# 1/den of a linear attention: from broadcasts into 32 partitions to broadcasts into all 128 from four stored copies

## Chip, cores and metric

The kernel runs on one core of one Trainium2 chip. The metric is device time in microseconds (us) for one execution; the time before is the median of three runs.

## What is computed

A block of a transformer, for 2048 rows of width 1024: a layer norm with a modulation taken from a conditioning vector `c`, linear attention with 32 heads of 32 columns, a residual sum, a second modulated layer norm, a gated feed-forward part of inner width 3584, and a second residual sum. The change lies in the attention:

```python
phi = lambda t: jnp.where(t > 0, t + 1, jnp.exp(t)) + 1e-06
pq, pk = (phi(q), phi(k))
kv = jnp.einsum('bhsd,bhse->bhde', pk, v)
z = jnp.einsum('bhsd->bhd', pk)
num = jnp.einsum('bhqd,bhde->bhqe', pq, kv)
den = jnp.einsum('bhqd,bhd->bhq', pq, z)[..., None] + 1e-06
o = num / den
return (lambda x, *d: x.transpose(*d))(o, 0, 2, 1, 3).reshape(B, S, D) @ wo
```

`den` is one number for each head and row. Inputs and outputs are bf16.

## The kernel before

The 2048 rows are 16 chunks of 128 (`NCH`) in four groups of 512 (`sg`, 0 to 3). The 1024 columns are eight groups of 128 (`g`, 0 to 7), each with four heads of 32 columns. `PQ[sg]` holds phi(q) transposed: its 128 partitions are the columns of one head group, so that partition 32k to 32k+31 belongs to head k of the group; its free dimensions are `g` and the row.

1/den is needed in that layout: the same value on the 32 partitions of a head. The kernel gets it in these steps.

- `den(pr_, b)` (L1233 on) treats two row groups together (`pr_` 0: groups 0 and 1; 1: groups 2 and 3). TensorE multiplies `PQ` by a masked `z` into one PSUM bank, VectorE adds 1e-6 (L1245) and takes the reciprocal into `RDC` (L1246). `RDC` has 128 partitions of 256 f32, one kilobyte each. A DMA stores it to the DRAM tensor `scr_rd` (L1248).
- `rb_load(sg, hs)` (L1255) reads it back for a row group, half by half (`h`; half a group is 256 rows). For each head of a group, one DMA reads a row of 8 KB (eight head groups of 256 f32) and writes it to 32 partitions of `RB[sg % 2]`: four DMAs of 256 KB for each half, 32 in all (L1260).
- `pq_scale(sg, h, gs)` (L1268) multiplies `PQ` by `RB` in place on VectorE, two head groups at a time (L1273), four multiplies for each half.
- `wo_mm` (L1283) multiplies the scaled `PQ` by `W2`, the product of kv and the output weights; VectorE adds the residual (L1291).

Before `wo_mm` TensorE works through 24 tiles of pk times the normalised input (`m_tile`, L895). When the third tile of a head group is evacuated by ScalarE (L900), `m_t(g)` transposes it by DMA (L703, into `mtb`), `kv_prod(g)` multiplies it on TensorE (L913), VectorE masks the result into `kvt` (L920), and `w2_pair(i)` makes `W2` for two head groups on TensorE (L1201), copied by ScalarE and VectorE (L1208).

The order on TensorE and on the DMA queue of SyncE (SP) is that of the program. A table `HOOK` says after which tile a step is put:

```python
HOOK = {0: "ga", 6: "kv0", 10: "kv1", 11: "w0", 13: "kv2", 15: "modp kv3 z32", 16: "den0", 17: "w1 rb0.0 rb0.1", 18: "",
        19: "kv4", 20: "den1 ps0.0", 21: "gbr", 22: "ps0.1", 23: "rb2.0"}
```

After the tiles come the rest of the loads (`rb_load(1)`, `rb_load(2, (1,))`, L1356 and L1357), then the chunks of `wo_mm`, and between these the loads and multiplies of row group 3 and the steps of the second layer norm (`SLOT`).

The order on VectorE, ScalarE and GpSimd between two marks of the program (L1050 and L1765) is chosen by a planner, `reorder` (L244): it computes a due time for every operation backwards, from estimated costs and the dependencies, DMAs included, and then places the ready operation that is due first. Dependencies between operations, through SBUF, PSUM or stated by hand, become semaphore waits. The DMAs of SP use eight semaphores in turn, and each DMA waits for the one eight places before it.

Of the kernel before, what the change touches and what calls it, by code (L numbers as in the profile page):

```python
# [10 lines left out]
P = 128  # L11
# [3 lines left out]
NSG = 4  # L15
CPG = NCH // NSG
SGW = P * CPG
NDC = D // P
NG = 8
HPG = 4  # L20
# [310 lines left out]
def bass_adaLN_cond__linear_attn_block__geglu_ffn__prompt_kernel(  # L331
# [12 lines left out]
    bf16, f32, f32r, i32 = dt.bfloat16, dt.float32, dt.float32r, dt.int32  # L344
# [1 line left out]
    scr_mod = nc.dram_tensor("scr_mod", [2, NDC, P], f32).ap()  # L346
    scr_y = nc.dram_tensor("scr_y", [4 * CPG, P, NDJ, 2 * P], bf16).ap()
    scr_x = nc.dram_tensor("scr_x", [P, NCH, D], bf16).ap()
    scr_rd = nc.dram_tensor("scr_rd", [NSG, 2, HPG, NG, SGW // 2], f32).ap()
    with ExitStack() as es:  # L350
        es.enter_context(nc.allow_non_contiguous_dma(reason="1024 modulation values, laid out by partition"))
        arena = es.enter_context(nc.sbuf_tensor("arena", [P, ARENA_BYTES], dt.uint8, align_bytes=64))
# [4 lines left out]
        def at(name, shape, dty, off):  # L357
            return nc.alloc_sbuf_tensor_at(name, shape, dty, offset=ABASE + off, align_bytes=4)
# [39 lines left out]
        RB = [at(f"rb{i}", [P, 2, NG, SGW // 2], f32, OFF_RB[i]) for i in range(2)]  # L398
# [39 lines left out]
        RDC = _small["rdc"]  # L438
# [6 lines left out]
        def r_sm(name):  # L445
            return [(SMO[name], SMO[name] + SMSZ[name], name)]
# [30 lines left out]
        def r_wv(g):  # L477
            return [(OFF_WK + g * 2048, OFF_WK + (g + 1) * 2048, "wv")]
# [4 lines left out]
        def r_pq(sg, k0=0, k1=NG, s0=0, s1=SGW):  # L483
            return r_t8(PQO[sg], f"pq{sg}", k0, k1, s0, s1)
# [46 lines left out]
        def r_rb(i, h, g0=0, g1=NG):  # L531
            return [(OFF_RB[i] + (h * NG + g0) * 1024, OFF_RB[i] + (h * NG + g1) * 1024, f"rb{i}")]
# [19 lines left out]
        sch = Sched()  # L552
        T, A, V, G, Q = PE_, ACT_, DVE_, POOL_, SP_
# [12 lines left out]
        def pset_writer(b, o):  # L566
            for t_ in pr(b):
                sch.ps.set_writer(t_[0], t_[1], o)
# [49 lines left out]
        for q in range(1, 4):  # L618
            wmq_dma(q)
            for d0, d1 in ((2 * q, 2 * q + 1), (2 * q + 1, 2 * q + 2)):  # L620
# [8 lines left out]
               rd=r_sm("c8") + r_sm("ident"), pwr=pr(4))  # L629
# [4 lines left out]
               rd=r_sm("thc") + r_sm("chalf"), wr=r_sm("siluT"))  # L634
# [507 lines left out]
        for c_ in range(10, NCH):  # L1142
            b = seq.index(("k", c_ // 2 * 2, 0)) - (9 if c_ % 2 else 12)
# [6 lines left out]
        for c_ in range(8, NCH, 2):  # L1150
            b = seq.index(("k", c_, 0)) - 3
# [10 lines left out]
        for g in range(NG):  # L1162
            task(nk + g // 2, lambda g=g: sch.dma(Q, lambda e: e.dma_start(WV[:, g, :, :], wqkv_v[:, :, 2 * D + g * P:2 * D + (g + 1) * P]),
                                                  wr=r_wv(g), note=f"wv{g}"))
# [3 lines left out]
        def ga_pass():  # L1168
            b = 6
            mod_rows(((0, 2, b, hl_src),))  # L1170
            o_r = mod_store(2, b, MROW0, [(XHO[2], XHO[2] + 1024, "mrow0")], 0)
            row_load(GAB, R_GAB, 0, 0, "gab", o_r)
# [60 lines left out]
        HW = SGW // 2  # L1233

        def den(pr_, b):
            o = None
            for g in range(NG):
                for i in range(4):
                    sg, t0 = 2 * pr_ + i // 2, (i % 2) * HW
                    o = sch.op(T, lambda e, g=g, i=i, sg=sg, t0=t0: e.matmul(  # L1240
                        ps_all[32 * i:32 * (i + 1), b * 512:b * 512 + HW], Z32[:, g, :], PQ[sg][:, g, t0:t0 + HW],
                        start=(g == 0), stop=(g == NG - 1)),
                        rd=r_sm("z32") + r_pq(sg, g, g + 1, t0, t0 + HW), pwr=(pr(b) if g == 0 else ()), note=f"den{pr_} {g}.{i}")
            pset_writer(b, o)
            sch.op(V, lambda e: e.tensor_scalar(RDC[:, :], PS(b, 0, HW), 1e-6, None, op0=ALU.add), prd=pr(b), wr=r_sm("rdc"), note=f"dene{pr_}")  # L1245
            sch.op(V, lambda e: e.reciprocal(RDC[:, :], RDC[:, :]), rd=r_sm("rdc"), wr=r_sm("rdc"), note=f"rden{pr_}")  # L1246
            def store():
                o_rd[pr_] = sch.dma(Q, lambda e: e.dma_start(scr_rd[2 * pr_:2 * pr_ + 2].rearrange("s f k g t -> (s f k g) t"), RDC[:, :]),  # L1248
                          rd=r_sm("rdc"), note=f"rden{pr_}.st")
            return store  # L1250

        o_rd = {}
        rb_ops = {}

        def rb_load(sg, hs=(0, 1)):  # L1255
            i = sg % 2
            for h in hs:
                made = []
                for k in range(HPG):
                    made.append(sch.dma(Q, lambda e, h=h, k=k: e.dma_start(  # L1260
                        RB[i][32 * k:32 * (k + 1), h, :, :].rearrange("p a b -> p (a b)"),
                        scr_rd[sg, h, k:k + 1, :, :].rearrange("k g t -> k (g t)").to_broadcast([32, NG * HW])),
                        wr=r_rb(i, h) if k == 0 else (), deps=made[0].deps if k else [o_rd[sg // 2]], note=f"rb{sg}.{h}.{k}"))
                rb_ops[sg, h] = made

        GH = [((0, 2), (2, 4)), ((4, 6), (6, 8))]

        def pq_scale(sg, h, gs):  # L1268
            i, t0 = sg % 2, h * HW
            for g0, g1 in gs:  # L1270
                ap = PQ[sg][:, g0:g1, t0:t0 + HW]
                rng = r_pq(sg, g0, g1, t0, t0 + HW)
                sch.op(V, lambda e, ap=ap, i=i, h=h, g0=g0, g1=g1: e.tensor_tensor(ap, ap, RB[i][:, h, g0:g1, :], ALU.mult),  # L1273
                       rd=rng + r_rb(i, h, g0, g1), wr=rng, deps=rb_ops[sg, h], note=f"pqs{sg}.{h}.{g0}")

        x1_ops, s_ops = {}, {}

        def wo_mm(c_, b0, gs):
# [9 lines left out]
            if gs[-1] == NG - 1:  # L1288
# [10 lines left out]
        wo_load(1)  # L1299
        NWO = 5  # L1300
        tiles = [(g, k) for g in range(4) for k in range(3)] + [(g, 0) for g in range(4, NG)] + [(g, k) for g in range(4, NG) for k in (1, 2)]
        HOOK = {0: "ga", 6: "kv0", 10: "kv1", 11: "w0", 13: "kv2", 15: "modp kv3 z32", 16: "den0", 17: "w1 rb0.0 rb0.1", 18: "",
                19: "kv4", 20: "den1 ps0.0", 21: "gbr", 22: "ps0.1", 23: "rb2.0"}
        st = {}

        def hook_run(f):
            if f[:2] == "kv":
                kv_prod(int(f[2:]), 4)
            elif f == "ga":
                ga_pass()  # L1310
            elif f == "gbr":
                assert mdone[0] == 64
                gb_rows()
            elif f == "modp":
                mod_pass()
            elif f == "z32":
                z32()
            elif f[:3] == "den":
                st[int(f[3:])] = den(int(f[3:]), 5)
                st[int(f[3:])]()  # L1320
            elif f[:2] == "ps":
                pq_scale(int(f[2]), int(f[4]), GH[0] + GH[1])
            elif f[:2] == "rb":
                rb_load(int(f[2]), (int(f[4]),))
            elif f[0] == "w":
                w2_pair(int(f[1:]))

        for n, (g, k) in enumerate(tiles):
# [16 lines left out]
            if n == 11:  # L1345
                gb_load(1, 0)
                gb_load(1, 1)
            for f in HOOK.get(n, "").split():
                hook_run(f)
# [476 lines left out]
        for n in range(12):  # L1826
            q, i = divmod(n, 4)
# [6 lines left out]
        for u in range(2 * NFP):  # L1834
# [5 lines left out]
            else:  # L1840
                a = ACTS.get(u, ((), ()))
# [143 lines left out]
```

## Time and profile before

| | |
|---|---|
| time, median of 3 runs (lowest to highest) | 783.16 us (782.22 to 784.1) |
| profiled execution, span (the profile gives no total beside it) | 780.9 us |
| TensorE busy | 770.2 us, 99% |
| VectorE busy | 645.9 us, 83% |
| ScalarE busy | 374.6 us, 48% |
| GpSimd busy | 47.5 us, 6% |
| granted TensorE clock | 1.000 |
| loads of 1/den (L1260) | 32 of 256 KB, first issue at 176.7 us, last at 236.4; median 6.0 us to landing |
| stores of 1/den (L1248) | 2 of 128 KB, at 174.4 and 185.7 us |
| multiplies by 1/den (L1273) | 32 of 684 ns, 185.6 to 247.7 us |

A row of an engine's timeline gives start, duration, line, operation, output and inputs, the number of operations, and in brackets how long the engine stood idle before it and for what. "PE" is TensorE, "DVE" VectorE, "ACT" ScalarE, "POOL" GpSimd, "SPq" the DMA queue of SyncE. Times are counted from the start of the span.

### The profile page before, as it was taken

How to read it: one execution, taken by the hardware profiler on the slowest of the kernel's cores; microseconds unless marked ns; L12 is line 12 of the kernel's file. 1: busy time of each engine (PE TensorE's matmuls, PEld its weight loads, DVE VectorE, ACT ScalarE, POOL GpSimd, SP SyncE). 2: the span in 40 equal slices, each digit the busy share in tenths (PEclk: the TensorE clock that was granted, in tenths of full speed). 3: DMA queues.
4: the chain of work that ended last, by engine and by line, in shares of the span. 5: the costliest groups of instructions: out<-in, count | busy, mean ns of one | idle time of the engine just before them, and what ended most of it. 6: DMA issues, size and time to landing. Idle time of an engine off the chain costs nothing.

```text
span 780.9 us, 10753 instructions
## 1 busy us (share of the span) xinstructions
PE 770.2 (99%) x3825; PEld 496.2 (64%) x3883; DVE 645.9 (83%) x964; ACT 374.6 (48%) x629; POOL 47.5 (6%) x126
## 2 busy tenths in 40 slices
PE   8999999999999999999999999999999999999998
PEld 4444445666445667667676767667676576677766
DVE  6699988897899878787989888888989888676767
ACT  2497743242466487878755555555555211111111
POOL 2031300000321011100000000000000000000000
PEclk9999999999999999999999999999999999999999
DMA  9879749939999358867353865535356334443331
GB/s 284 256 167 252 158 91 215 255 80 196 203 287 231 82 138 212 230 175 215 99 145 108 250 211 172 148 96 161 97 147 221 111 127 139 144 141 114 126 125 60
DMA packets 196940, 130.22 MB, mean 167 GB/s; under 512 B 69516, under 2 KB 182420, under 8 KB 195864
## 3 DMA queue, kind: packets, MB, share of 16 engines
q1 hardware_dynamic: 196872, 129.55, 62.4%
q8 instruction: 30, 0.49, 0.3%
q14 instruction: 22, 0.18, 0.1%
q10 hardware_dynamic: 16, 0.00, 0.0%
HBM read 92.55 MB, written 23.35 MB: 148 GB/s over the span
## 4 chain that ended last, share of the span: by engine, by line
PE 95%; SPq 2%; DMA 1%; DVE 1%; issue 1%; ACT 0%; DVEq 0%; ACTq 0%
PE ps_all L1458 45%; PE ps_all L1672 21%; PE ps_all L895 7%; PE ps_all L934 7%; PE ps_all L1283 7%; PE ps_all L880 5%; PE ps_all L1593 1%; SPq L598 1%; DMA wmq<-in_w_mod_dram 1%; SPq L603 1%; DMA h1T<-xh 0%; PE ps_all L913 0%; PE ps_all L1201 0%; PE ps_all L1240 0%; DVE h1T L724 0%
## 5 line engine op out<-in xcount | busy, mean ns | idle before, releaser
L1458 PE MATMUL ps_all<-ss,tp 128*128 128x512 f32 x896 | 214.3, 396 | 0.0
L1458 PEld LDWEIGHTS ps_all<-ss,tp 128*128 128x128 f32 x896 | 168.3, 188 | 37.8 <-DVE ss L1413 0.2
L1672 PE MATMUL ps_all<-dt,sb 128*128 128x512 f32 x424 | 102.5, 398 | 0.0
L1481 ACT ACTIVATE ge<-ps_all 128x512 f32<-128x512 f32 x112 | 64.1, 597 | 73.8 <-DVE ps_all L1469 62.1
L1458 PE MATMUL ps_all<-h2a,wt 128*128 128x512 bf16 x421 | 95.7, 379 | 1.8
L1672 PEld LDWEIGHTS ps_all<-dt,sb 128*128 128x128 f32 x424 | 79.6, 188 | 18.5 <-DVE sb L1648 0.3
L1476 DVE TENSOR_TENSOR ps_all<-ps_all,es 128x512 f32<-128x512 f32 x54 | 37.6, 699 | 49.4 <-ACT es L1466 49.0
L1488 DVE TENSOR_TENSOR ys<-ge,ps_all 128x512 bf16<-128x512 f32 x112 | 74.4, 684 | 3.8 <-PE ps_all L1672 0.5
L1458 PEld LDWEIGHTS ps_all<-h2a,wt 128*128 128x128 bf16 x448 | 38.0, 98 | 57.3 <-ACT ps_all L1463 16.9
L1433 DVE TENSOR_TENSOR tp<-wt 128x1024 fp32r<-128x1024 bf16 x56 | 68.1, 1217 | 1.8 <-DMA wt<-in_B_w_up_dram 1.8
L1433 DVE TENSOR_TENSOR tp<-wt,tp 128x1024 fp32r<-128x1024 bf16 x56 | 68.2, 1218 | 0.0
L934 PE MATMUL ps_all<-h1T,wq 128*128 128x512 bf16 x256 | 56.7, 379 | 0.0
L880 PE MATMUL ps_all<-wk,h1T 128*128 128x512 bf16 x239 | 55.3, 379 | 1.1 <-DMA wk<-in_A_wqkv_dram 0.5
L1283 PE MATMUL ps_all<-w,pq 128*128 128x512 bf16 x249 | 55.7, 379 | 0.5 <-issue 0.2
L1458 PE MATMUL ps_all<-ar,tp 128*128 128x512 f32 x224 | 55.5, 390 | 0.0
L869 ACT ACTIVATE eb<-ps_all 128x512 f32<-128x512 f32 x64 | 36.3, 594 | 37.6 <-PE ps_all L880 16.0
L1672 PE MATMUL ps_all<-wd,ya 128*128 128x512 bf16 x199 | 47.5, 380 | 0.7
L1458 PEld LDWEIGHTS ps_all<-ar,tp 128*128 128x128 f32 x224 | 42.1, 188 | 8.9
L1463 ACT ACTIVATE ps_all<-ps_all 128x512 f32<-128x512 f32 x56 | 32.6, 582 | 26.8 <-PE ps_all L1458 26.5
L934 PEld LDWEIGHTS ps_all<-h1T,wq 128*128 128x128 bf16 x256 | 25.0, 98 | 30.0
L1283 PEld LDWEIGHTS ps_all<-w,pq 128*128 128x128 bf16 x256 | 24.6, 98 | 30.3 <-issue 1.1
L1643 ACT ACTIVATE sb<-ya 128x896 fp32r<-128x896 bf16 (+1 forms) x16 | 14.5, 913 | 58.8 <-PE ps_all L1672 58.8
(141 smaller groups left out, 976.3 us busy)
## 6 DMA issues: line engine op xcount, KB each, us to landing
wt<-in_B_w_gate_dram SPq DMA_DIRECT2D x28, 512.0 KB, 4.0
wt<-in_B_w_up_dram SPq DMA_DIRECT2D x28, 512.0 KB, 5.2
scr_y<-ys SPq DMA_DIRECT2D x28, 512.0 KB, 3.2
ya<-scr_y SPq DMA_DIRECT2D x14, 896.0 KB, 4.9
rb<-scr_rd SPq DMA_DIRECT2D x32, 256.0 KB, 6.0
wd<-in_B_w_down_dram SPq DMA_DIRECT2D x7, 1024.0 KB, 7.6
wmst<-in_w_mod_dram SPq DMA_DIRECT2D x6, 1024.0 KB, 6.2
wmq<-in_w_mod_dram SPq DMA_DIRECT2D x8, 512.0 KB, 7.5
```

The lines of the kernel that those rows point to most:

```text
L869: sch.op(A, lambda e: e.activation(EB[i][:, :], PS(bank), ACTF.Exp), prd=pr(bank), wr=rng, note=f"{note}.exp")
L880: o = sch.op(T, lambda e, dc=dc: e.matmul(PS(bank), H1[sg][:, ci, dc, :], W_[:, dc, jg * 512:(jg + 1) * 512], start=(dc == 0), stop=(dc == ...
L895: o = sch.op(T, lambda e, c_=c_: e.matmul(PS(bank, 0, n), PK[c_][:, g * P:(g + 1) * P], xrow(c_, o_, o_ + n), start=(c_ == 0), stop=(c_ == ...
L934: o = sch.op(T, lambda e, dc=dc: e.matmul(PS(b), WQ[:, dc, qc * P:(qc + 1) * P], H1[sg][:, :, dc, :], start=(dc == 0), stop=(dc == NDC - 1 ...
L1283: last[half] = sch.op(T, lambda e, g=g, half=half: e.matmul(PS(b0 + half), PQ[sg][:, g, ci * P:(ci + 1) * P], W2[:, g, half * 512:(half + ...
L1433: sch.op(V, lambda e: e.tensor_tensor(TP[k][:], in0, in1 if k in (0, 2) else in1[:], ALU.subtract), rd=r0 + r1, wr=r_tp(k), deps=[x1_ops[7 ...
L1458: o = sch.op(T, lambda e, l_=l_, r_=r_, dc=dc: e.matmul(PS(b), l_, r_, start=fresh and dc == 0, stop=dc == ND2 - 1, skip_group_check=True) ...
L1463: sch.op(A, lambda e: e.activation(PS(BB + t), PS(BA + t), ACTF.Copy), prd=pr(BA + t), pwr=pr(BB + t), note="pcp")
L1476: sch.op(V, lambda e: e.tensor_tensor(PS(BC + t), PS(BC + t), ES[t][:, :], ALU.add), prd=pr(BC + t), rd=r_2k(OFF_ES[t], f"es{t}"), pwr=pr( ...
L1481: sch.op(A, lambda e: e.activation(GE[i][:, :], PS(b), ACTF.Gelu_apprx_tanh), prd=pr(b), wr=r_2k(OFF_GE[i], f"ge{i}"), note="gelu")
L1488: sch.op(V, lambda e: e.tensor_tensor(YS[s_][:, 2 * h:2 * h + 2, t, :], q(GE[i][:, :]), q(PS(b + 1)), ALU.mult), rd=r_2k(OFF_GE[i], f"ge{i ...
L1672: o = sch.op(T, lambda e, l_=l_, r_=r_, j=j, dst=dst: e.matmul(dst, l_[:, 0, :], r_, start=(k in (1, 5) or own is not None) and j == js[0] ...
```

## The change

`scr_rd` gets a dimension of four copies (`NRP`). The store becomes four DMAs, one for each copy. A load covers all 128 partitions and two head groups, in rows of 2 KB: its source is 16 rows (4 heads x 4 copies), each of which goes to eight partitions. There are again four DMAs of 256 KB for each half. A multiply now depends on the load of its own two head groups, where it depended on all four loads of the half. The first four multiplies are made to depend on the second reciprocal. In `HOOK` the stores are steps of their own: the first goes from tile 16 to tile 17, the second from tile 20 to tile 22.

```diff
-    scr_rd = nc.dram_tensor("scr_rd", [NSG, 2, HPG, NG, SGW // 2], f32).ap()
+    NRP = 4
+    scr_rd = nc.dram_tensor("scr_rd", [NSG, 2, HPG, NRP, NG, SGW // 2], f32).ap()
...
-            sch.op(V, lambda e: e.reciprocal(RDC[:, :], RDC[:, :]), rd=r_sm("rdc"), wr=r_sm("rdc"), note=f"rden{pr_}")
+            rd_ops[pr_] = sch.op(V, lambda e: e.reciprocal(RDC[:, :], RDC[:, :]), rd=r_sm("rdc"), wr=r_sm("rdc"), note=f"rden{pr_}")
             def store():
-                o_rd[pr_] = sch.dma(Q, lambda e: e.dma_start(scr_rd[2 * pr_:2 * pr_ + 2].rearrange("s f k g t -> (s f k g) t"), RDC[:, :]),
-                          rd=r_sm("rdc"), note=f"rden{pr_}.st")
+                o_rd[pr_] = [sch.dma(Q, lambda e, r=r: e.dma_start(scr_rd[2 * pr_:2 * pr_ + 2, :, :, r, :, :].rearrange("s f k g t -> (s f k) g t"), RDC[:, :]),
+                                     rd=r_sm("rdc"), note=f"rden{pr_}.st") for r in range(NRP)]
...
             for h in hs:
-                made = []
-                for k in range(HPG):
-                    made.append(sch.dma(Q, lambda e, h=h, k=k: e.dma_start(
-                        RB[i][32 * k:32 * (k + 1), h, :, :].rearrange("p a b -> p (a b)"),
-                        scr_rd[sg, h, k:k + 1, :, :].rearrange("k g t -> k (g t)").to_broadcast([32, NG * HW])),
-                        wr=r_rb(i, h) if k == 0 else (), deps=made[0].deps if k else [o_rd[sg // 2]], note=f"rb{sg}.{h}.{k}"))
-                rb_ops[sg, h] = made
+                for g0 in range(0, NG, 2):
+                    src = scr_rd[sg, h, :, :, g0:g0 + 2, :].rearrange("k r g t -> (k r) (g t)").unsqueeze(1).to_broadcast([HPG * NRP, P // (HPG * NRP), 2 * HW])
+                    sch.dma(Q, lambda e, h=h, g0=g0, src=src: e.dma_start(
+                        RB[i][:, h, g0:g0 + 2, :].rearrange("p a b -> p (a b)"), src),
+                        wr=r_rb(i, h, g0, g0 + 2), deps=o_rd[sg // 2], note=f"rb{sg}.{h}.{g0}")
...
-                       rd=rng + r_rb(i, h, g0, g1), wr=rng, deps=rb_ops[sg, h], note=f"pqs{sg}.{h}.{g0}")
+                       rd=rng + r_rb(i, h, g0, g1), wr=rng, deps=[rd_ops[1]] if sg + h == 0 else [], note=f"pqs{sg}.{h}.{g0}")
...
-        HOOK = {0: "ga", 6: "kv0", 10: "kv1", 11: "w0", 13: "kv2", 15: "modp kv3 z32", 16: "den0", 17: "w1 rb0.0 rb0.1", 18: "",
-                19: "kv4", 20: "den1 ps0.0", 21: "gbr", 22: "ps0.1", 23: "rb2.0"}
+        HOOK = {0: "ga", 6: "kv0", 10: "kv1", 11: "w0", 13: "kv2", 15: "modp kv3 z32", 16: "den0", 17: "w1 st0 rb0.0 rb0.1", 18: "",
+                19: "kv4", 20: "den1 ps0.0", 21: "gbr", 22: "ps0.1 st1", 23: "rb2.0"}
...
-                st[int(f[3:])]()
+            elif f[:2] == "st":
+                st[int(f[2:])]()
```

More of the change, by code (lines that the diff above doesn't have):

```diff
@@ L1245, in den @@
             sch.op(V, lambda e: e.tensor_scalar(RDC[:, :], PS(b, 0, HW), 1e-6, None, op0=ALU.add), prd=pr(b), wr=r_sm("rdc"), note=f"dene{pr_}")
-            sch.op(V, lambda e: e.reciprocal(RDC[:, :], RDC[:, :]), rd=r_sm("rdc"), wr=r_sm("rdc"), note=f"rden{pr_}")
+            rd_ops[pr_] = sch.op(V, lambda e: e.reciprocal(RDC[:, :], RDC[:, :]), rd=r_sm("rdc"), wr=r_sm("rdc"), note=f"rden{pr_}")
             def store():
-                o_rd[pr_] = sch.dma(Q, lambda e: e.dma_start(scr_rd[2 * pr_:2 * pr_ + 2].rearrange("s f k g t -> (s f k g) t"), RDC[:, :]),
-                          rd=r_sm("rdc"), note=f"rden{pr_}.st")
+                o_rd[pr_] = [sch.dma(Q, lambda e, r=r: e.dma_start(scr_rd[2 * pr_:2 * pr_ + 2, :, :, r, :, :].rearrange("s f k g t -> (s f k) g t"), RDC[:, :]),
+                                     rd=r_sm("rdc"), note=f"rden{pr_}.st") for r in range(NRP)]
             return store
         o_rd = {}
-        rb_ops = {}
+        rd_ops = {}
         def rb_load(sg, hs=(0, 1)):
```

## The prediction

> **What bounds the kernel now.** I read the page's busy times and chain first, then the DMA queue's rows around the change, then what the loads wait for and who waits for them.
>
> ```profile
> PE 770.2 (99%) x3825; PEld 496.2 (64%) x3883; DVE 645.9 (83%) x964; ACT 374.6 (48%) x629; POOL 47.5 (6%) x126
> ...
> PE 95%; SPq 2%; DMA 1%; DVE 1%; issue 1%; ACT 0%; DVEq 0%; ACTq 0%
> ...
> rb<-scr_rd SPq DMA_DIRECT2D x32, 256.0 KB, 6.0
> ```
>
> TensorE is busy 99% of the span and is 95% of the chain that ended last. No load of 1/den is on that chain. A gain can only come from TensorE's idle time near the change; a loss can come from anything that newly reaches TensorE late. The windows of 2 us from 164 to 248 us add up to 84.00 us, of which TensorE is busy 83.58: at most 0.42 us can be won there.
>
> The DMA queue (SP) in order of time; columns are start, duration, operation:
>
> ```profile
> 174.40 0.81 SPq L1248 DMA_DIRECT2D scr_rd<-rdc  x1
> 175.32 1.27 SPq L703 DMA_TRANSPOSE mtb<-mb  x1
> 176.69 3.76 SPq L1260 DMA_DIRECT2D rb<-scr_rd  x8
> 180.55 1.23 SPq L703 DMA_TRANSPOSE mtb<-mb  x1
> 185.74 0.35 SPq L1248 DMA_DIRECT2D scr_rd<-rdc  x1
> 186.20 2.16 SPq L703 DMA_TRANSPOSE mtb<-mb  x1
> 188.45 0.56 SPq L849 DMA_DIRECT2D scr_row<-mrg  x1
> 191.15 1.26 SPq L703 DMA_TRANSPOSE mtb<-mb  x1
> 192.51 12.38 SPq L1260 DMA_DIRECT2D rb<-scr_rd  x16
> ```
>
> The store of the first 1/den, the transpose for head group 4, eight loads of 256 KB, the transpose for group 5; then the second store, the transposes for groups 6 and 7, sixteen loads. Windows of 2 us while the loads run (the last two columns are the DMA share and GB/s):
>
> ```profile
> 198.00:200.00 2.00, 2.00 (x11) 0.88 (x9) 0.55 (x2) 0.11 (x1) 0.00 (x0) 1.00 1.03 225
> 200.00:202.00 2.00, 2.00 (x11) 0.93 (x10) 1.78 (x4) 0.00 (x0) 0.00 (x0) 1.00 1.03 225
> 232.00:234.00 2.00, 2.00 (x11) 0.93 (x10) 2.00 (x4) 1.13 (x3) 0.00 (x0) 1.00 1.13 360
> ```
>
> The loads fill the DMA engines at 225 GB/s, where other transfers at about the same share move 360. Last, VectorE and TensorE around the point of use:
>
> ```profile
> 188.74 2.50 DVE L1273 TENSOR_TENSOR pq<-pq,rb 128x512 bf16<-128x512 bf16 x4 [0.73 <-DMA rb<-scr_rd]
> ...
> 199.83 1.89 DVE L1273 TENSOR_TENSOR pq<-pq,rb 128x512 bf16<-128x512 bf16 x3 [1.45 <-DMA rb<-scr_rd]
> ```
> ```profile
> 190.42 0.61 PE L913 MATMUL ps_all<-mtb,wv 128*128 128x128 bf16 x8
> ...
> 194.57 1.05 PE L913 MATMUL ps_all<-mtb,wv 128*128 128x128 bf16 x16
> ```
>
> VectorE waits for loads 2.2 us in all; TensorE follows without a gap in either place. The sharpest date is the first of the two TensorE rows: it needs the transpose for group 5, whose weights load at 190.28 and whose transpose landed 9.0 us after its issue at 180.55, so at 189.6. That transpose stands in the queue behind the eight loads.
>
> **First store and its eight loads.** The store moves behind the transpose for group 4 and becomes four of 128 KB. ScalarE ends that transpose's input at 174.49, so the transpose is issued at about 174.6 instead of 175.32 and ends at 175.9. Two stores are on record, with issues of 0.35 and 0.81 us; with 0.08 between issues, the last of four starts at 177.2 to 178.6, middle 177.9. The store at 174.40 landed after 2.2 us. The four copies overlap (each queued load is issued 0.4 to 0.5 us after the last and doesn't wait for its landing), so the first load is issued at 179.4 to 180.8, middle 180.1, against 176.69: 3.4 us later.
>
> The first of the eight loads landed 3.6 us after issue (180.3), the eighth, issued at 180.0, 8.6 us after (188.6): 1.19 us each. The last load therefore lands 2.4 us plus eight spacings after the first issue. The new spacing is not on record for this shape. Its bounds: 1.19 us (no change) and 0.72 us (2 KB rows of the input over 128 partitions at 2 to 4 us into the span: 279 GB/s at a share of 0.77, so 362 GB/s at a full share). In between lie the gate and up weights in quiet stretches, 512 KB landing 1.74 us apart (265.66 + 3.9 and 266.2 + 5.1), 0.87 us for 256 KB, in rows of 512 B. I take 0.72 us, the row with the same row length and partitions. It is supported by the broadcast row of 512 KB over 128 partitions at 134.6 us, which landed in 3.8 us where half as many bytes of 1/den took 3.6.
>
> [...]
>
> With 0.72 the eighth load lands 2.4 + 5.8 = 8.2 us after the first issue, at 188.3, and the transpose behind it 1.0 us later (as before: 188.6 and 189.6), at 189.3, bounds 188.6 to 190.0. It is needed at 190.28: no wait, with 0.3 to 1.7 us to spare. Break-even is a spacing of 0.84 us. At 0.87 TensorE waits at most 0.9 us.
>
> VectorE: the multiplies now wait for one load each. The first four start after the second reciprocal (185.6) as before, when four loads have landed (185.4 in the middle case), so the new dependency on that reciprocal costs nothing. The next four follow at 188.0 without the 0.73 us wait and end by 190.7 instead of 191.2. The masking of group 5 behind them comes no later, so no new wait for TensorE's next step at 192.7.
>
> **Second store.** It moves behind the transpose for group 6 and the row store at 188.45. SP no longer stands waiting for the reciprocal at 185.7. Transpose 6 goes at 186.05, ends at 187.3 to 188.2, the row store by 188.0 to 188.9, four stores of 0.43 to 0.89 us by 189.7 to 192.5, middle 191.0. The transpose for group 7 can't start before 191.15 in either kernel. In the middle it is unmoved; at the worst end it slips 1.4 us and lands at 195.6, where the second half of the 16 multiplies at 194.57 wants it at 195.0: 0.6 us. The sixteen loads begin when the last store has landed, 192.2 to 193.9 against 192.51. Their first four end 5.3 us later, 197.5 to 199.2 against 199.7, when VectorE is free at 198.4: most of its 1.45 us wait goes. What is late next is TensorE: the residual sums behind it had waited 0.22 us for it at 201.94, so little is passed on.
>
> **The rest.** The loads hold the DMA engines 32 x 0.47 = 15 us less; six more stores give back some 6 x 0.55 = 3.3 us (128 KB at about 230 GB/s). The transfers that this sets free are weights and transposes in stretches where TensorE never waits: hidden, and worth nothing unless that cover goes. Multiplies are the same in number and size.
>
> **Sum.** 780.9 us span, 0 added on TensorE in the middle case, 0.42 won at most, 0.9 + 0.6 lost at most while loads speed up. The profiled execution shows no time beside its span; the median of the runs, 783.16, is 2.26 us above it, which I carry over. Forecast 783.2 us.
>
> **Rivals.**
> - Slower: the loads don't speed up (limited by reading the same rows, or by too few engines), while they start 3.4 us later. At 1.19 us the transpose for group 5 lands at 193.0, TensorE waits 2.8 us: 786.0. It decides from 0.84 us a load. For it: no such transfer of this table is in the trace. Against: 279 to 360 GB/s of other transfers over 128 partitions. 0.08.
> - Slower: the four stores don't overlap, 4 x 2.2 us. Loads begin at 184.8, the transpose lands at 194.0: 3.7 us, 786.9. Against: the loads' landings 1.19 us apart. 0.03. [...]
> - Slower: the planner (L244) reads the DMAs and their dependencies, so VectorE's order shifts within its stretch. One 1.22 us operation put ahead of the masking of a group costs TensorE 0.9 to 1.2 us; with a second one 2.4 us, 785.6. Against: PE has no wait of 1 us in this stretch, so the order has some room. 0.05 for over 0.2%.
> - Faster: a better order or an emptier DMA queue removes idle time. In the stretch 0.42 us gives 782.7, which is still no change. Beyond 0.2% it would have to come from somewhere I can't see: 0.05.
>
> **How the numbers follow.** About 0.2%, 1.6 us, is what a measurement of this kernel can tell from no change (its runs spread from 782.22 to 784.1). My forecast with its bounds (782.7 to 784.7) and the small gain have 0.79; the slower cases 0.16; faster 0.05. The range takes in the runs' spread below the 782.7, to 782.0, and above it the forecast's 784.7 and the milder part of the slower cases, to 785.0; the two late-start cases, near 786 and 787, and a hidden gain are left out, at some 0.18.
>
> **What would show it.** Right: loads of 1/den landing about 0.7 us apart, some 360 GB/s in their windows; first load near 180.1; the group 5 transpose landed before TensorE's L913 row at 190.4, which stays there; VectorE's waits for rb near zero; span within 1 us. Wrong: a wait of TensorE for mtb near 190 or 195, load landings 1.2 us apart, or VectorE's order changed with new waits of TensorE behind it. A span shorter by over 1 us would refute that TensorE alone sets the time.

## The result and the profile after

The changed kernel takes 786.79 us (median of five runs, 785.74 to 787.29) against 782.59 us for the kernel before (782.22 to 784.1): a ratio of 1.0048, 95% interval 1.0036 to 1.0060. It is 4.2 us slower. The forecast of 783.2 us, no change beyond some 0.2%, was wrong, and the time lies above the predicted range, 782.0 to 785.0. A second measurement on another chip (e12 below) gives 1.0053 (1.0037 to 1.0070). The profiled execution spans 784.0 us, 3.1 more than the one before; with a total of 785.74 us it is the fastest of the five. Why the others are some 1 us longer is taken up by the last experiment.

From the page of the kernel after, the lines that answer to those of before:

```profile
PE 770.6 (98%) x3825; PEld 497.0 (63%) x3883; DVE 646.1 (82%) x964; ACT 374.5 (48%) x629; POOL 47.6 (6%) x126
...
PE 92%; SPq 3%; DMA 3%; DVE 1%; issue 1%; DVEq 0%; ACT 0%
...
rb<-scr_rd SPq DMA_DIRECT2D x32, 256.0 KB, 6.4
```

The work is the same: TensorE is busy 770.6 us where it was 770.2. The chain that ended last has changed: the DMA engines hold 3% of it where they held 1%, and TensorE 92% where it held 95%. The chain itself says where:

```profile
182.81 0.85 PE ps_all L896 x5
183.65 0.05 SPq L1261
183.75 0.60 SPq L1261
184.39 0.60 SPq L1261
185.09 8.34 DMA mtb<-mb
193.57 0.61 PE ps_all L914 x8
```

Columns are start and duration. The chain leaves TensorE at 183.7 us, goes through the last two issues of loads of 1/den (L1261) and the transpose for head group 5 behind them, which takes 8.3 us to land, and comes back to TensorE at 193.57. The timeline of TensorE has the same place, with the idle time in brackets:

```profile
188.85 1.47 PE L896 MATMUL ps_all<-xall,pk 128*128 128x342 bf16 x9
193.57 0.61 PE L914 MATMUL ps_all<-mtb,wv 128*128 128x128 bf16 x8 [3.24 <-DMA mtb<-mb]
```

3.24 us of idle time against 3.1 us of span: this one wait is the whole loss of the profiled execution. In the kernel before, the same row stood at 190.42 with no wait. The DMA queue in order:

```profile
174.26 1.26 SPq L704 DMA_TRANSPOSE mtb<-mb  x1
175.57 2.53 SPq L1249 DMA_DIRECT2D scr_rd<-rdc  x4
179.94 5.04 SPq L1261 DMA_DIRECT2D rb<-scr_rd  x8
185.09 5.64 SPq L704 DMA_TRANSPOSE mtb<-mb  x2
190.83 0.54 SPq L850 DMA_DIRECT2D scr_row<-mrg  x1
191.47 3.02 SPq L1249 DMA_DIRECT2D scr_rd<-rdc  x4
194.65 1.29 SPq L704 DMA_TRANSPOSE mtb<-mb  x1
```

What the reader is to see, with the landing times from the trace's DMA records:

- **The start.** Four stores are issued in 2.53 us, 0.60 us each; each lands 2.4 us after its own issue, so that they overlap. The last is issued at 177.5 and lands at 179.9, and the first load follows at 179.94. The prediction had 180.1.
- **The loads.** They land at 184.6 (second), 186.7 (fourth), 189.0, 189.6, 190.3 and 191.1 (eighth). From the second to the eighth that is 6.5 us for six, 1.08 us each in the mean, where the prediction took 0.72. The steps are uneven: 2.3 us lie between the fourth and the fifth, 0.6 to 0.8 between the later ones. The eighth is down 11.1 us after the first issue; before, this took 11.9 us, the prediction had 8.2.
- **The tail.** The transpose for group 5 lands at 193.4, 2.4 us after the eighth load, where before it was 1.0 us.

So the loads ahead of the transpose start 3.25 us later, 0.8 us come back from their faster landing, and 1.4 us are lost at the end: 3.8 us later than before (193.4 against 189.6). It had some 0.7 us to spare before, when its weights were loaded at 190.28; now TensorE needs it by about 190.2.

The windows of 2 us with the second batch of loads in them (last two columns DMA share and GB/s) show the rate directly:

```profile
202.00:204.00 2.00, 2.00 (x11) 0.87 (x9) 1.89 (x4) 0.00 (x0) 0.00 (x0) 1.00 0.89 259
204.00:206.00 2.00, 2.00 (x11) 0.92 (x10) 1.12 (x2) 0.00 (x0) 0.00 (x0) 1.00 0.83 301
```

259 to 301 GB/s, against 225 before: better, and far from the 360 that the prediction wanted. In the windows of the first batch, 182 to 190 us, it is 208 to 282. VectorE, last, waits for loads about as long as before (2.0 us in two waits; 2.2 before):

```profile
189.06 2.72 DVE L1272 TENSOR_TENSOR pq<-pq,rb 128x512 bf16<-128x512 bf16 x4 [1.09 <-DMA rb<-scr_rd]
...
200.25 0.69 DVE L1272 TENSOR_TENSOR pq<-pq,rb 128x512 bf16<-128x512 bf16 x1 [0.90 <-DMA rb<-scr_rd]
```

### The profile page after: what moved, and what is told of

The parts are those of the page before. It is cut to its first block, busy times and chain, and to the rows that moved or that the text cites. A ratio compares the mean times of both kernels' runs of the same rounds, so it can differ in the third digit from the quotient of the medians.

```text
span 784.0 us, 10757 instructions
## 1 busy us (share of the span) xinstructions
PE 770.6 (98%) x3825; PEld 497.0 (63%) x3883; DVE 646.1 (82%) x964; ACT 374.5 (48%) x629; POOL 47.6 (6%) x126
## 4 chain that ended last, share of the span: by engine, by line
PE 92%; SPq 3%; DMA 3%; DVE 1%; issue 1%; DVEq 0%; ACT 0%
PE ps_all L1458 42%; PE ps_all L1672 21%; PE ps_all L935 7%; PE ps_all L1282 7%; PE ps_all L896 6%; PE ps_all L881 6%; SPq L599 2%; PE ps_all L1593 1%; DMA mtb<-mb 1%; DMA scr_x<-xall 1%; SPq L604 1%; DMA wk<-in_A_wqkv_dram 1%; DVE tp L1433 1%; PE ps_all L914 0%; PE ps_all L1202 0%
```

## The experiments

All times are medians, set against the kernel before on the same chip (782.8 to 783.1 us in each case). Diffs are against the changed kernel unless said otherwise.

**The two halves of the change, each alone.** In e1 1/den is stored once, at its old place, and the loads keep their new form: 16 rows of 2 KB over 128 partitions. The sixteen rows are the four heads' rows of 8 KB cut in four, the same for every load of a half, so that the partitions get 1/den of other head groups. Number and size of the pieces are those of the change; the addresses are others, since there is one copy and not four.

```diff
-    scr_rd = nc.dram_tensor("scr_rd", [NSG, 2, HPG, NRP, NG, SGW // 2], f32).ap()
+    scr_rd = nc.dram_tensor("scr_rd", [NSG, 2, HPG, NG, SGW // 2], f32).ap()
...
-                    src = scr_rd[sg, h, :, :, g0:g0 + 2, :].rearrange("k r g t -> (k r) (g t)").unsqueeze(1).to_broadcast([HPG * NRP, P // (HPG * NRP), 2 * HW])
+                    src = scr_rd[sg, h].rearrange("k (c g) t -> (k c) (g t)", g=2).unsqueeze(1).to_broadcast([HPG * NRP, P // (HPG * NRP), 2 * HW])
...
-        HOOK = {... 16: "den0", 17: "w1 st0 rb0.0 rb0.1", ... 20: "den1 ps0.0", 21: "gbr", 22: "ps0.1 st1", 23: "rb2.0"}
+        HOOK = {... 16: "den0 st0", 17: "w1 rb0.0 rb0.1", ... 20: "den1 st1 ps0.0", 21: "gbr", 22: "ps0.1", 23: "rb2.0"}
```

> The new loads alone: one store at its old place before the transpose for group 4, loads over 128 partitions in rows of 2 KB. The 16 source rows are the 8 KB rows of the four heads cut in four (one copy only, so the values that a multiply gets belong to other heads and head groups; the output is not the reference's). Theory (the loss comes from the later start of the first eight loads, with the transpose for group 5 queued behind them): the first load is issued near 176.7 us, the eighth lands about 11 us later at 187.8, the group 5 transpose by 190.2, TensorE waits at most 0.2 us, time 782.2 to 783.4, as before. Rival (the new form of load itself costs the time): a wait of TensorE for mtb of 2 to 3 us stays, 785 to 787.

Measured: 783.02 us, ratio 1.0001 (0.9992 to 1.0011). DMA queue and TensorE of e1:

```profile
176.71 5.11 SPq L1261 DMA_DIRECT2D rb<-scr_rd  x8
181.92 1.25 SPq L704 DMA_TRANSPOSE mtb<-mb  x1
```
```profile
190.78 0.61 PE L914 MATMUL ps_all<-mtb,wv 128*128 128x128 bf16 x8
```

The first load is at its old place (176.69 before), the landings are 1.00 us apart (180.1 to 187.1), the transpose for group 5 lands at 188.0, 0.9 us behind the last load, and TensorE's row has no bracket: no wait. The new loads alone cost nothing, and as TensorE sets the time here, they also bring nothing.

In e2 the four stores at their new places stay, and the loads, with the multiplies' dependence on all four of a half, are the old ones, from the first copy:

```diff
-                for g0 in range(0, NG, 2):
...
+                for k in range(HPG):
+                    made.append(sch.dma(Q, lambda e, h=h, k=k: e.dma_start(
+                        RB[i][32 * k:32 * (k + 1), h, :, :].rearrange("p a b -> p (a b)"),
+                        scr_rd[sg, h, k:k + 1, 0, :, :].rearrange("k g t -> k (g t)").to_broadcast([32, NG * HW])),
```

> The new stores alone: four stores at their new places, loads as before (32 partitions, rows of 8 KB) from the first copy. Theory (late start): the first load is issued near 179.9 us, the eighth lands 11.9 us later at 191.8, the group 5 transpose 1 to 2.4 us behind it, TensorE waits 2.6 to 4 us for it, time 785.2 to 787. Rival (the new loads are the cause): no wait over 0.5 us, time 782.2 to 783.4.

Measured: 788.71 us, ratio 1.0080 (1.0065 to 1.0095): slower, as the theory says, but 1.7 us over the upper end expected. Queue and TensorE of e2:

```profile
180.01 3.62 SPq L1261 DMA_DIRECT2D rb<-scr_rd  x8
183.74 7.70 SPq L704 DMA_TRANSPOSE mtb<-mb  x2
```
```profile
194.42 1.01 PE L914 MATMUL ps_all<-mtb,wv 128*128 128x128 bf16 x8 [4.05 <-DMA mtb<-mb]
```

The four stores at their new places bring the loss (5.8 us), the new loads give about a third of it back (788.71 to 786.79). The wait is 4.05 us, the span 6.0 us longer than before; the rest is found at the end of this section.

**Is it the move or the fourfold store?** e7 is e1 with the places of the change: one store, after the transpose for group 4. The diff is against e1.

```diff
-        HOOK = {... 16: "den0 st0", 17: "w1 rb0.0 rb0.1", ... 20: "den1 st1 ps0.0", 21: "gbr", 22: "ps0.1", 23: "rb2.0"}
+        HOOK = {... 16: "den0", 17: "w1 st0 rb0.0 rb0.1", ... 20: "den1 ps0.0", 21: "gbr", 22: "ps0.1 st1", 23: "rb2.0"}
```

> As the run with the new loads alone (one copy, 16 rows cut from it), but with the one store at the changed kernel's places, behind the transpose for group 4. Theory (the start of the first eight loads sets the loss, in proportion): the first load is issued near 178.4 us, between 176.7 and 179.9; the eighth lands some 10.4 us later at 188.8, the transpose for group 5 1.0 us behind it at 189.8, or 2.4 us at 191.2 if the fetch of instructions falls into it; TensorE waits 0 to 1 us, time 782.5 to 784.0. Rival (moving the store, not making four of it, is the whole loss): 785.5 or more.

Measured: 783.2 us, ratio 1.0002 (0.9992 to 1.0011). The queue and TensorE of e7:

```profile
176.06 0.57 SPq L1249 DMA_DIRECT2D scr_rd<-rdc  x1
178.07 5.10 SPq L1261 DMA_DIRECT2D rb<-scr_rd  x8
183.27 4.78 SPq L704 DMA_TRANSPOSE mtb<-mb  x2
```
```profile
190.65 0.61 PE L914 MATMUL ps_all<-mtb,wv 128*128 128x128 bf16 x8
```

The first load is 1.4 us later than before, and the transpose arrives at 190.5, with no bracket behind TensorE's row: just in time. The move uses up the margin. In the changed kernel the transpose lands 3.0 us later than here. Of these, 1.9 us are the three further stores (the first load at 179.94 instead of 178.07), and 1.0 us is that the eight loads then take 11.1 us from the first issue to the last landing, and here 10.2. In two further runs (e12, e11) eight loads from four copies took 10.7 and 10.8 us, and in e1 eight from one copy took 10.4. So the copies made the loads no faster; why they were slower is not shown.

e11 does the reverse: the changed kernel, four stores, at the old places.

```diff
-        HOOK = {... 16: "den0", 17: "w1 st0 rb0.0 rb0.1", ... 20: "den1 ps0.0", 21: "gbr", 22: "ps0.1 st1", 23: "rb2.0"}
+        HOOK = {... 16: "den0 st0", 17: "w1 rb0.0 rb0.1", ... 20: "den1 st1 ps0.0", 21: "gbr", 22: "ps0.1", 23: "rb2.0"}
```

> The changed kernel with its four stores at the old places: ahead of the transpose for group 4, and straight behind the second reciprocal. Theory (what counts is the DMA work ahead of a transpose): four stores are issued from 174.2 to 176.8 us, the transpose for group 4 lands near 180.0 and TensorE, which needs it at 178.9, waits 1.0 us; the first load is issued near 178.8, the transpose for group 5 lands at 190.6 to 192 against a need of 191: 0 to 1 us more. Time 783.6 to 785.2, between the kernel before and the changed one. Rival (the move of the stores is what costs): as before, 782.2 to 783.4.

Measured: 784.2 us, ratio 1.0019 (1.0010 to 1.0029). Queue and TensorE of e11:

```profile
174.39 2.54 SPq L1249 DMA_DIRECT2D scr_rd<-rdc  x4
177.04 1.32 SPq L704 DMA_TRANSPOSE mtb<-mb  x1
```
```profile
180.26 0.61 PE L914 MATMUL ps_all<-mtb,wv 128*128 128x128 bf16 x8 [0.96 <-issue]
```

Now the transpose for group 4 stands behind the four stores; it lands at 180.2, and TensorE, which needs it, has waited 0.96 us (the profile calls the wait "issue" here; the landing time says what it was). Group 5 comes in time. The first four stores cost 2.5 us of the queue at the one place as at the other (2.54 here, 2.53 in the changed kernel), each time ahead of a transpose that is needed.

**Can the queue's order be mended?** e4 puts the second four loads behind the transpose for group 5.

```diff
-        HOOK = {... 17: "w1 st0 rb0.0 rb0.1", 18: "", 19: "kv4", ...}
+        HOOK = {... 17: "w1 st0 rb0.0", 18: "", 19: "rb0.1 kv4", ...}
```

> The changed kernel, with the four loads of the second half put behind the transpose for group 5 instead of ahead of it. Theory (queue order): the transpose is issued near 182.6 us and lands before 190, TensorE has no wait for mtb; what is late next is VectorE, whose second four multiplies wait for the later loads and keep the masking of group 5 back: 0 to 1.2 us, time 782.4 to 784.0. Rival (the transpose is late for another reason, such as the fetch of instructions by DMA near 190 us): a wait for mtb of over 1 us stays, 785 or more.

Measured: 784.59 us, ratio 1.0021 (1.0012 to 1.0030), 0.6 us over the upper end expected. The wait for group 5 is gone (landed 187.9), another has come:

```profile
188.90 3.30 SPq L1249 DMA_DIRECT2D scr_rd<-rdc  x4
192.69 1.24 SPq L704 DMA_TRANSPOSE mtb<-mb  x1
```
```profile
196.44 0.62 PE L914 MATMUL ps_all<-mtb,wv 128*128 128x128 bf16 x8 [1.21 <-DMA mtb<-mb]
```

The transpose for group 7 now stands behind the second four stores, and TensorE waits 1.21 us for it. That confirms that the wait for group 5 is made by the queue's order, and refutes that nothing is late after the mending. e9 puts the second stores ahead of the transpose for group 6 as well (the diff is against e4):

```diff
-                19: "rb0.1 kv4", 20: "den1 ps0.0", 21: "gbr", 22: "ps0.1 st1", ...}
+                19: "rb0.1 kv4", 20: "den1 st1 ps0.0", 21: "gbr", 22: "ps0.1", ...}
```

> The kernel with the transpose for group 5 ahead of the second half's loads, and the second four stores put back ahead of the transpose for group 6, where SP stood idle before. Theory (what was left there, 1.2 us of waiting for the transpose for group 7, comes from the four stores issued just ahead of it): transposes 6 and 7 are issued near 189.5 and 191.4, TensorE waits under 0.4 us, time 782.4 to 783.4. Rival (transposes behind four stores are late wherever the stores stand): a wait of 1 us or more, 784 to 785.

Measured: 784.26 us, ratio 1.0021 (1.0011 to 1.0030): what the rival said, a transpose behind four stores is late here too. TensorE of e9 waits for the transposes of groups 6 and 7, 1.4 us together:

```profile
195.41 0.62 PE L914 MATMUL ps_all<-mtb,wv 128*128 128x128 bf16 x8 [1.07 <-DMA mtb<-mb]
196.32 0.62 PE L914 MATMUL ps_all<-mtb,wv 128*128 128x128 bf16 x8 [0.30 <-DMA mtb<-mb]
```

e10 takes the second stores out of the transposes' way altogether: behind all of them, with the later loads and the multiplies of row group 2 moved back to suit.

```diff
-        HOOK = {... 17: "w1 st0 rb0.0 rb0.1", 18: "", 19: "kv4", 20: "den1 ps0.0", 21: "gbr", 22: "ps0.1 st1", 23: "rb2.0"}
+        HOOK = {... 17: "w1 st0 rb0.0", 18: "", 19: "rb0.1 kv4", 20: "den1 ps0.0", 21: "gbr", 22: "ps0.1"}
...
-            rb_load(2, (1,))
+            st[1]()
+            rb_load(2)
...
-        pq_scale(2, 0, GH[0] + GH[1])
...
-                 4: lambda: (cb1(), wt_dma(0)),
+                 4: lambda: (cb1(), wt_dma(0), pq_scale(2, 0, GH[0] + GH[1])),
```

> Four copies and the new loads, but nothing of them queued ahead of a transpose that TensorE waits for: the transpose for group 5 between the two halves of the first loads, the second four stores behind the transpose for group 7 and behind the loads of row group 1, and the multiplies of the first half of row group 2 two chunks later, so that VectorE does not stand waiting for them. Theory (the whole loss is DMA work ahead of the transposes): no wait of TensorE for mtb over 0.3 us, time 782.2 to 783.3, as before, and no better, since TensorE has no other idle time here. Rival (the copies cost something else as well): 784 or more with no wait for mtb, or a new wait for the multiplies of row groups 1 and 2.

Measured: 784.07 us, ratio 1.0016 (1.0006 to 1.0027). No wait for a transpose is left. TensorE's waits from 150 to 262 us hold a new one of 0.5 us for the second layer norm's sums:

```profile
PE ps_all L1459 <- DVE ss L1414: 0.5, 2, 0.3
```

The theory's 782.2 to 783.3 is missed, and the mark set for the rival has come: 784 or more with no wait for a transpose. So waits for the transposes are not all that this order costs. Of the 1.0 us, 0.5 is located, and the rest is open; so is whether it comes from the stores or from the loads and multiplies that were moved for them. No order that I tried makes the four stores free, and none beats the kernel before, whose TensorE has no wait above 0.2 us here that better loads could take away.

**Why the loads did not reach 0.72 us.** e5 keeps the shape on the SBUF side and the row length, and reads 128 different rows (of the input `x`) where the change reads 16 rows eight times each. The store and the places are those of e1. One execution; the values in `RB` are not 1/den.

```diff
-                    src = scr_rd[sg, h, :, :, g0:g0 + 2, :].rearrange("k r g t -> (k r) (g t)").unsqueeze(1).to_broadcast([HPG * NRP, P // (HPG * NRP), 2 * HW])
+                    src = x_v[:, ((sg * 2 + h) * 4 + g0 // 2) % NCH, :]
...
-                        RB[i][:, h, g0:g0 + 2, :].rearrange("p a b -> p (a b)"), src),
+                        RB[i][:, h, g0:g0 + 2, :].rearrange("p a b -> p (a b)").bitcast(bf16), src),
```

> As the run with the new loads alone, but each load reads 128 different rows of 2 KB of the input x instead of 16 rows eight times each (the multiplies get rows of x instead of 1/den; the output is not the reference's). Theory (the loads are slow because the same rows are read again and again): landings 0.6 to 0.75 us apart in the batch of sixteen, 340 to 420 GB/s. Rival (the limit is on the side of SBUF or in the number of packets): 0.9 to 1.0 us apart, 260 to 290 GB/s, as with 1/den. Time about 782.6 in both.

Measured: 783.15 us; landings 0.80 us apart in the first batch (180.2 to 185.8) and 0.78 in the second, between the theory's 0.6 to 0.75 and the rival's 0.9 to 1.0. Most neighbours are about 0.7 us apart; a few longer gaps raise the mean. Windows of e5 and, below them, of e1:

```profile
198.00:200.00 2.00, 2.00 (x11) 0.90 (x10) 2.00 (x4) 0.60 (x1) 0.00 (x0) 1.00 0.98 365
200.00:202.00 2.00, 2.00 (x11) 0.88 (x9) 0.67 (x2) 0.00 (x0) 0.00 (x0) 1.00 1.01 333
```
```profile
200.00:202.00 2.00, 2.00 (x11) 0.93 (x10) 0.54 (x1) 0.00 (x0) 0.00 (x0) 1.00 1.06 262
```

At about the same DMA share, 333 to 365 GB/s with different rows and 262 with sixteen rows read eight times each. So row length and partitions alone do not set the spacing. That it is the repeated reading as such is not shown: e5 also reads another tensor, and its pattern has 128 rows in front where e1 has 16, so that the pieces may fall to the DMA engines in another way. The packets of 2 KB differ between e1 and the changed kernel too. In the first eight loads half of them take 131 ns or more in e1; in the changed kernel and in e5 the median is 84 ns, but in the changed kernel single ones take up to 951 ns.

e6 asks the counter-question of the old loads: 32 different rows of 8 KB (of `w_mod`) into 32 partitions, the rest as in the kernel before; again the values are not 1/den, and it is one execution. The diff is against the kernel before.

```diff
-                        RB[i][32 * k:32 * (k + 1), h, :, :].rearrange("p a b -> p (a b)"),
-                        scr_rd[sg, h, k:k + 1, :, :].rearrange("k g t -> k (g t)").to_broadcast([32, NG * HW])),
+                        RB[i][32 * k:32 * (k + 1), h, :, :].rearrange("p a b -> p (a b)").bitcast(bf16),
+                        w_mod[32 * (((sg * 2 + h) * 4) + k):32 * (((sg * 2 + h) * 4) + k + 1), 0:2 * NG * HW]),
```

> The kernel before, with loads of 32 different rows of 8 KB of w_mod into 32 partitions instead of one row 32 times (the multiplies get weights instead of 1/den; the output is not the reference's). Theory (32 partitions limit the load, on the side of SBUF): landings stay 1.15 to 1.25 us apart, 220 GB/s. Rival (reading one row again and again is the limit): 0.75 to 0.9 us apart, 300 GB/s or more.

Measured: 782.44 us, landings 1.19 us apart as with one row read 32 times, and

```profile
198.00:200.00 2.00, 2.00 (x11) 0.90 (x10) 0.69 (x2) 0.00 (x0) 0.00 (x0) 1.00 1.05 225
```

So the old loads were not limited by the repeated reading; what is left is their form, 32 partitions with rows of 8 KB, of which no run changed one alone. Into all 128 partitions more came through than these 225 GB/s: the mean of the first batch of e5 is 328 (256 KB in 0.80 us), its best window of 2 us (202 to 204) shows 404, and the repeated rows of e1 262.

e8 is what the four copies avoid: one store at the old place, and each load broadcasts four rows to 32 partitions each.

```diff
-                    src = scr_rd[sg, h, :, :, g0:g0 + 2, :].rearrange("k r g t -> (k r) (g t)").unsqueeze(1).to_broadcast([HPG * NRP, P // (HPG * NRP), 2 * HW])
+                    src = scr_rd[sg, h, :, g0:g0 + 2, :].rearrange("k g t -> k (g t)").unsqueeze(1).to_broadcast([HPG, P // HPG, 2 * HW])
```

> New loads without copies: one store, each load reads 4 rows of 2 KB (one for each head), each for 32 partitions. [...] Rival (16 engines as with 16 rows): 1.0 us a load, 782.5 to 783.5, and the four copies buy nothing.

Measured: 829.8 us in one execution, against the rival's 782.5 to 783.5, which is refuted. A window with the loads, and TensorE's two largest waits over the whole span of e8:

```profile
184.00:186.00 2.00, 2.00 (x21) 1.07 (x20) 1.97 (x3) 0.84 (x2) 0.00 (x0) 1.00 0.26 102
```
```profile
PE ps_all L1282 <- DVE pq L1272: 15.2, 8, 4.7
PE ps_all L914 <- DMA mtb<-mb: 11.1, 1, 11.1
```

A DMA share of 0.26, as much as four of the 16 engines busy throughout, at 102 GB/s. e1, with one store at the same place and 16 rows in front, eight partitions each, has 1.06 and 256 GB/s in the same window. Whether it is the number of rows in front or the 32 readings of each that makes the difference, this run does not show. It shows why the change reads 16 rows, for which it makes its copies, and their stores are what costs. (Of the 47 us, the two waits are 26.3, and the granted clock, 0.981 over 828 us, another 15.7; the last experiment shows how the two hang together.)

**The microsecond that the first profile does not have.** Its wait explains 3.1 us; the medians are 4.2 us apart. The granted clock of that execution was 1.000, that of the four others of the first measurement 0.997 to 0.998. e12 is the changed kernel, unedited, for a second profile.

> The changed kernel as it is, for a second profiled execution. The first one had a TensorE wait of 3.24 us for the transpose of group 5, a granted clock of 1.000 and a span of 784.0 us; four other executions without a profile had clocks of 0.997 to 0.998 and spans of 784.6 to 785.5. The kernel with four stores and the old loads, which waits 4.05 us there, shows a clock of 0.60 and 0.55 in the two windows of 2 us behind its wait. Theory: the wait is the direct loss, and in most executions it also lets the clock fall to half for about 3.6 us behind it, which costs about 1.7 us more (1.0 us in the mean of spans). Then this profile shows either a wait near 3.2 us with windows of about 0.5 to 0.6 behind it and a span of 785 to 785.6, or, as in one of five before, full clock and a span of 784.0. Median 786 to 787.3. Rival: the further 1 us of the median has nothing to do with this place; then the clock behind the wait is 1.00 also where the span is 785 or more, and the missing clock lies somewhere else in the span.

Measured: 787.41 us, ratio 1.0053 (1.0037 to 1.0070); the profiled execution spans 785.7 us at a clock of 0.998. Median and span are each 0.1 us above the theory's ranges. Its waits and windows (the third figure from the end of a row is the granted clock):

```profile
PE ps_all L914 <- DMA mtb<-mb: 2.9, 1, 2.9
```
```profile
190.00:192.00 2.00, 0.58 (x4) 0.17 (x2) 1.33 (x2) 0.46 (x1) 0.00 (x0) 1.00 1.38 80
192.00:194.00 2.00, 0.54 (x7) 0.57 (x8) 0.00 (x0) 0.00 (x0) 0.00 (x0) 0.91 0.91 214
194.00:196.00 2.00, 1.78 (x8) 0.89 (x7) 0.45 (x2) 0.00 (x0) 0.00 (x0) 0.50 0.76 201
196.00:198.00 2.00, 2.00 (x14) 0.49 (x12) 0.00 (x0) 0.00 (x0) 0.00 (x0) 0.74 0.64 122
```

TensorE waits 2.9 us, and then runs at half clock until about 197.5. The missing clock of the three windows is (0.09 + 0.50 + 0.26) x 2 us = 1.7 us; everywhere else in the span it is 1.00. 2.9 of wait, 1.7 of clock and the 0.2 us of issue that TensorE waits longer than before make 4.8, and the span is 4.8 us longer than the one before (785.7 against 780.9). e2 shows the same behind its wait of 4.05 us:

```profile
194.00:196.00 2.00, 1.36 (x9) 1.13 (x11) 0.99 (x3) 0.00 (x0) 0.00 (x0) 0.60 0.90 232
196.00:198.00 2.00, 2.00 (x6) 0.71 (x5) 0.00 (x0) 0.00 (x0) 0.00 (x0) 0.55 0.90 200
```

(0.40 + 0.45) x 2 = 1.7 us again. Cut at the points where the clock changed, the windows of e12 are:

```profile
190.23:193.64 3.41, 0.53 (x7) 0.21 (x5) 1.33 (x2) 0.46 (x1) 0.00 (x0) 1.00 1.14 132
193.64:197.05 3.41, 3.19 (x14) 1.55 (x13) 0.45 (x2) 0.00 (x0) 0.00 (x0) 0.50 0.88 211
```

Half clock lasts 3.41 us, in e2 too (194.40 to 197.81). In e8 it lasts 3.41 us or two or four times that, and its five falls within the program, at 192.69, 223.41, 240.48, 264.37 and 298.51 us, lie 9, 5, 7 and 10 times 3.41 us apart. So in e8 the clock changes on a grid of 3.41 us, and the 3.41 us of e12 and e2 agree with it. In the last 3.41 us before the clock fell, TensorE was busy 0.53 us in e12, not at all in e2, and 0.80 us before the first fall of e8. Waits of 0.96 to 1.2 us (e4, e9, e11) left the clock of the profiled executions at 1.000 (one execution of e9 without a profile, 786.51 us, shows 0.998), and the first profile of the changed kernel kept it through 3.24 us. A wait that the grid cuts in two, so that neither stretch is as idle as these, would explain this; it is not shown, since where the grid lay in that execution is not on record. The stretch ahead of a fall need not be idle throughout: a wait of 2.9 us was enough in e12, with TensorE busy for 0.53 us of the 3.41.

## Why the prediction was wrong, by its own steps

**Right.** The start: four stores cost SP what was worked out, and the first load is issued at 179.94 us (180.1 predicted). The stores overlap, each landing 2.4 us after its issue, so the rival of 786.9 us fell; that the median came out close to its time is an accident. The date is right: the transpose for group 5 is the first thing that TensorE misses. The planner kept its order but for one multiply put ahead of one copy, with no wait behind it: that rival fell too. Loads alone are worth nothing (e1), since TensorE sets the time.

**The step that failed** is the wait for the transpose of group 5: no wait was predicted, with 0.3 to 1.7 us to spare, and TensorE waited 3.24 us. The transpose was to land at 189.3 and landed at 193.4. The start of the loads was 0.2 us better than predicted; the spacing of the loads took 2.9 us more, and the tail, the time from the last load's landing to the transpose's, 1.4 more.

**Wrong: the spacing of the loads.** The step took 0.72 us for 256 KB, from a row with the same length and partitions, put the break-even at 0.84, and measured are 1.08 (0.98 in e12, 1.00 in e1). This is the term that turns the sign: with 0.72 the eighth load would have landed at 179.94 + 2.4 + 5.8 = 188.1, 3.0 us before the 191.1 measured. The row that was taken reads different rows; e5, with different rows, gives 0.80, so that 0.2 to 0.3 us of each load go with what e5 changed, the repeated reading among it. The row was also no clean one: 0.77 and 279 GB/s are the window from 3 to 4 us (2 to 4 us has 0.72 and 266), and it holds packets of 512 B beside those of 2 KB. The broadcast row at 134.6 us that was called in support took 3.8 us where half as many bytes of 1/den took 3.6; by the prediction's own sum 2.4 of these 3.6 us do not depend on the spacing, so a single landing says little of the spacing of queued loads. The rival "the loads don't speed up", at 1.19, had the right mechanism and place (786.0 us, a wait of 2.8 at 190), and was given 0.08. That its 2.8 comes near the 3.24 is in part luck: its spacing is too large, and the tail that it lacks makes up for it. With the bounds of the spacing at 0.72 and 1.19 and a break-even of 0.84 between them, three quarters of the unknown lay on the slow side; the chance was taken from the row believed, not from the bounds.

**Wrong: the tail.** The transpose was to land 1.0 us after the last load, as before; it was 2.4. It was 2.4 in e12 and e2 as well, and 2.2 in e7. With the measured tail even a spacing of 0.72 would have left TensorE a wait of 0.2 us. The cause stays open. A packet of 16 KB on the queue of instructions lies near these places, and it is a suspect: in the changed kernel (190.1), e12 (190.0) and e2 (191.7) it starts before the eighth load has landed, and in e4, e5, e9 and e10 the transpose lands before it starts, with tails of 1.0 to 1.1. But in the kernel before, e1, e6 and e7 it starts 0.3 us behind the last load in all four, and the tails are 1.0, 0.9, 1.0 and 2.2. One packet of 256 B that took 2.1 us started well before it (at 188.7 in the changed kernel). No run moved the packet of 16 KB alone.

**Right by luck: the second stores.** No second wait was predicted, and none came. The transpose for group 7, though, was issued at 194.65 us and landed at 197.8, where the prediction had 191.15 in the middle and a landing at 195.6 at worst; the sixteen loads began at 196.63 instead of 192.2 to 193.9. TensorE took it at 198.2 only because the wait for group 5 had made it over 3 us late; by the prediction's need, 195.0, it came 2.8 us too late. e4, where group 5 comes in time, shows the wait: 1.21 us for group 7.

**Missed: the clock.** The prediction and all its rivals priced a wait of TensorE at its own length. In the profiles of e12 and e2 the wait cost another 1.7 us of clock. Eight of the nine executions of the changed kernel had a granted clock of 0.997 or 0.998, so that most of them seem to have paid it; that is the likely reason that the medians stand 4.2 us apart and not 3.1. With it the rival of a spacing of 1.19 would have stood at 787.7.

**Wrong, without effect:** VectorE's waits for loads did not vanish (2.0 us for 2.2), since the loads came slower than predicted, and the sixteen later.

**Open:** half of the 1.0 us of e10, the cause of the longer tail, and why loads of rows read eight times are slower, from four copies more than from one (eight loads took 10.7 to 11.1 us, and 10.2 to 10.4).

## What to carry to other kernels

A transfer that gets faster is worth nothing where nobody waits for it, while what is put ahead of it in the same queue is paid by whatever stands behind: here three more stores of 0.6 us each, ahead of a transpose with 0.7 us to spare. When the price of a new transfer lies between two rows of the trace, work out the break-even first and take the chance from how much of the interval lies on either side; and take a row that agrees also in how the source rows are read, not only in length and partitions. A transfer that is in time may be so only because something else is late. An idle stretch of TensorE of about 3 us is to be priced with the clock that it may lose behind it, here 1.7 us in e12 and e2.

## What the runs showed of the hardware

- Loads of 256 KB over 128 partitions, in pieces of 2 KB, land 0.98 to 1.08 us apart when 16 rows are read eight times each (changed kernel, e12, e1), and 0.78 to 0.80 with 128 different rows (e5).
- Into 32 partitions 256 KB take 1.19 us, whether one row of 8 KB is read 32 times (kernel before) or 32 rows once (e6).
- With four source rows in front of the pattern (e8) the DMA share is 0.26, as much as four of 16 engines busy throughout, and the rate 102 GB/s; with 16 rows (e1) 1.06 and 256 GB/s in the same window, 184 to 186 us.
- The issue of a DMA on SP depends on its form: 0.60 us for a new load or one of the four stores; in the kernel before a load took 0.42, and 128 different rows in e5 0.42 too.
- After waits of 2.9 (e12) and 4.05 us (e2) TensorE ran at half clock for 3.41 us, a loss of 1.7 us; one wait of 3.24 us and those of about 1 us had no such effect. The falls of the clock in e8 lie whole multiples of 3.41 us apart.
